# Merged transposes and V loads, a two-pass value product, and a re-ranked instruction order in a thresholded attention and mixer kernel

## The chip, the cores and the metric

The kernel runs on one core of one Trainium2 chip. The metric is the device time of that core in microseconds (us); the time of a kernel is the median of its runs. A profile of one execution, taken by the hardware profiler, goes with it. Its span is a little different from the time of an unprofiled run.

Engines are named as in the profile: PE is TensorE's matmul part and PEld its weight loads, DVE is VectorE, ACT is ScalarE, POOL is GpSimd, SP is the synchronisation engine, which here only issues transfers.

## The reference

There are two parts. The first is attention with a threshold, for 8 batches of 8 heads, 576 rows and 64 columns a head, in fp32:

```python
scores = scale * np.matmul(q, k.transpose(0, 1, 3, 2))
thresh = np.max(scores, axis=-1, keepdims=True) - tau
scores = np.where(scores >= thresh, scores, -1e9)
attn = np.exp(scores - np.max(scores, axis=-1, keepdims=True))
attn = attn / (np.sum(attn, axis=-1, keepdims=True) + 1e-09)
x = np.matmul(attn, v)          # heads side by side: 576 x 512 a batch
```

The second is a mixer on each batch's `x`: a low-rank map over the 576 rows, `u = x + (U V)^T x` (rank 32), and a two-layer perceptron over the 512 columns, `out = u + relu(u W1) W2` with 2048 hidden columns.

## The kernel before, in words

**Tiling.** Two heads make a pair (64 + 64 columns fill the 128 partitions), 4 pairs a batch, 32 pairs in all. Rows come in tiles of 128; 576 = 4 x 128 + 64, so the last 64 rows of two neighbouring pairs share a fifth tile. This gives 9 score steps for two pairs and 144 in all (18 a batch).

**A score step** (`score_tasks`) computes the fp32 scores of one tile for two heads (L423, into two double PSUM banks). VectorE moves them out with the scale and their extreme (L439), ScalarE makes the threshold (L452) and the exponential (L460), VectorE selects and sums (L468) into one of 8 `w_ring` buffers. The weights must then be turned round for the value product. Most are turned by a transfer that SP issues (`turn`, L479); for the fifth tile it issues two, one for the 64 rows of each pair (L482), into columns 512 to 576 of each pair's `wT_ring` buffer. A few tiles are turned by PE with a copy by ScalarE (L487, L496).

**The value product** (`value_tasks`, L551) multiplies the turned weights with V, which is kept as two bf16 halves side by side, high and low (`vh`, L385 and L388). One matmul of 128 columns thus gives 64 columns of the high product and 64 of the low. ScalarE copies the low part out (L574), VectorE adds the high part (L578), GpSimd multiplies by the inverse of the sums (L585). Then come the low-rank map (L602, L617, L624) and the turning of `u` for the perceptron (L632, L641, L649).

**The perceptron** (`mixer_tasks`) of a batch is 16 up-products of 4 matmuls (L716) with a relu (L706), and for each row tile 4 groups of 4 down-products (L749), a sum (L758) and two stores (L771, L772). The fifth tiles of two batches are done together (L732, L775).

**Loads** (`load_tasks`). Q, K and V of a pair come as separate transfers per head and per half of the partitions, so V takes four (L322, L323; all are issued at L305). SP issues V's for the first batch, GpSimd afterwards. GpSimd also issues the weights W1 and W2 in 8 pieces each (L805, L808), cast to bf16 on the way, and all stores.

**The order.** No instruction is scheduled by hand. The class `Order` builds a static order for each engine: every piece of work is a `Task` with an engine, a cost, dependencies, an offset `off`, and for mixer work a due time `when`, counted in score steps. `run` walks a model of the engines and of two transfer queues and, at each point, takes among the tasks that could start within `PATIENCE` of the earliest the one with the smallest rank:

```python
def rank(c):
    s, t = c
    if t.when is not None:
        due = t.when <= steps + (1.0 if t.kind == kind else 0.0)
        return (t.when - 1000.0 if due else t.when + 1000000.0, s)
    return (t.ready + t.off, s)
```

So mixer work comes first once it is due and last before. Where the model sees PE idle for over 0.45 us it puts in matmuls on a tile of zeros (`fill`, L255). A weight piece can't be issued before the first score output of its own step, which `gate` names: W1 at steps 6, 8, ... 20 and W2 at 22, 24, ... 36 (L821, L823). The engines carry out the resulting lists strictly in order: a wait of one instruction holds all behind it on its engine.

Of the kernel before, what the change touches and what calls it, by code (L numbers as in the profile page):

```python
# [8 lines left out]
P = 128  # L9
# [11 lines left out]
HB = 64  # L21
NT = 5
NPAIR = H // 2
NP = B * NPAIR
EARLY = 8

# [15 lines left out]
class Task:  # L42
    __slots__ = ("engine", "cost", "fn", "deps", "off", "banks", "frees", "lag", "kind", "when", "dma",
                 "ndma", "steps",                  "left", "after", "ready", "at", "end", "got")

    def __init__(self, engine, cost, fn, deps=(), off=0.0, banks=0, frees=(), lag=0.0, kind=None,
                 when=None, dma=0.0, ndma=1, steps=0):
        self.engine, self.cost, self.fn = engine, cost, fn
        self.deps = [d for d in deps if d is not None]
        self.off, self.banks, self.frees, self.lag, self.kind = off, banks, frees, lag, kind  # L50
        self.steps = steps
        self.dma = dma
        self.ndma = ndma
        self.when = when
        self.after, self.ready, self.end, self.got = [], 0.0, None, []


class Order:
# [3 lines left out]
    PATIENCE = (0.15, 0.45, 0.15, 0.15, 0.15)  # L62
# [3 lines left out]
    LANDING = (3.0, 1.4)  # L66
    SWITCH = {"quadrants": 0.145, None: 0.095}
    PARTS = {"S": "quadrants"}

    def __init__(self, nbanks, filler):  # L70
        self.tasks, self.nbanks, self.filler = [], nbanks, filler

    def add(self, *args, **kw):
        t = Task(*args, **kw)
        self.tasks.append(t)
        return t

    def run(self):
# [11 lines left out]

# [13 lines left out]
        while left:  # L104
# [37 lines left out]
            at[e] = s + t.cost  # L142
            t.at, t.end = s, at[e] + t.lag
            if t.dma:
                q = e != POOL
                begin = max(moved[q], at[e] + 0.6)
                shared = min(t.dma, max(0.0, moved[1 - q] - begin))
                moved[q] = begin + t.dma + shared
                moved[1 - q] += shared
                t.end = moved[q] + self.LANDING[q]  # L150
                if not q:
                    lanes += [t.end] * t.ndma
# [14 lines left out]
def kernel(  # L167
# [50 lines left out]
    wT_ring = [wpool.tile([P, NT, 2, 640], BF16, name=f"wT_ring{n}") for n in range(2)]  # L218
    for t_ in wT_ring:
        nc.gpsimd.memset(t_[:, :, :, S:640], 0.0)  # L220
    vraw_ring = [wpool.tile([P, NT, 2, D], FP32, name=f"vraw_ring{n}") for n in range(2)]
    for t_ in vraw_ring:
        nc.gpsimd.memset(t_[HB:P, 4, :, :], 0.0)
# [41 lines left out]
    def head_rows(src, b, hp):  # L265
        return src[b, 2 * hp:2 * hp + 2].rearrange("j (p t) d -> p t j d", p=HB)
# [21 lines left out]
    def load_tasks(p, pr):  # L288
# [5 lines left out]
        def one(kind, e, part, to, of, j, deps):  # L294
            queue = {SP: nc.sync, SCA: nc.scalar, POOL: nc.gpsimd}[e]

            def fn(_):
                if kind == "v":
                    raw = pr.vraw
                else:  # L300
                    if pr.qkraw is None:
                        pr.qkraw = rawpool.tile([P, 9, 2, D], FP32, name="qkraw", tag="qkraw")
                    raw = pr.qkraw
                src = {"q": qv, "k": kv, "v": vv}[kind]
                queue.dma_start(raw[part, to, j, :], src[:, of, j, :])  # L305

            return add(e, 0.7, fn, deps, dma=0.2 if e == POOL else 0.35, off=20.0 if p else -9.0)
# [11 lines left out]
        for j in range(2):  # L319
            freed = [got("vlo", p - 2)]  # L320
            ev = SP if p < NPAIR else POOL
            loads["v"].append(one("v", ev, lo, slice(0, 5), slice(0, 5), j, freed))  # L322
            loads["v"].append(one("v", ev, hi, slice(0, 4), slice(5, 9), j, freed))  # L323
# [21 lines left out]
    def prepare_tasks(p):  # L345
# [3 lines left out]
        for x, (name, t0) in enumerate((("q", 0), ("k", 5))):  # L349
# [5 lines left out]
            task = add(PE, 0.44, turn_main, loads[name] + before, off=-2.0, banks=1, kind="qk")  # L355

            def copy(_, x=x, task=task):
# [5 lines left out]
            done[name + "T", p] = add(SCA, 0.55, copy, [task, got(name + "T", p - 1)], off=-1.0,  # L363
# [5 lines left out]
        task = add(PE, 0.11, turn_rest, loads["q"] + loads["k"] + before, off=-2.0, banks=1,  # L369
# [9 lines left out]
        done["qk4T", p] = add(SCA, 0.22, copy_rest, [task, got("qk4T", p - 1)], off=-1.0,  # L379
# [3 lines left out]
        def high(_):  # L383
            pr.vh = vpool.tile([P, NT, 2, 2, D], BF16, name="vh", tag="vh")
            nc.scalar.copy(out=pr.vh[:, :, :, 0, :], in_=pr.vraw)  # L385

        def low(_):
            nc.gpsimd.tensor_tensor(out=pr.vh[:, :, :, 1, :], in0=pr.vraw,  # L388
# [3 lines left out]
                                 loads["v"] + [got("AV", p - 2, g) for g in range(3)] + [got("vhi", p - 1)],  # L392
                                 off=3.0)
# [7 lines left out]
    def score_tasks(p, i):  # L401
# [8 lines left out]
        now = -20.0 if p < NPAIR else 0.0  # L410
# [20 lines left out]
        S_ = done["S", p, i] = add(PE, 0.97, scores, deps, off=now - 6.0, kind="S", steps=1)  # L431
# [4 lines left out]
        for x in range(2):  # L436
            def weigh(_, x=x):
# [6 lines left out]
            t = add(VEC, 0.69, weigh, [S_, got("w", tiles[0] + x - NS)],  # L444
                    off=now - 3.0 + 0.01 * x)
            done["P1", n, x] = t
            if x == 0 and n in gate:
                gate[n].deps.append(t)
# [6 lines left out]
        thr = add(SCA, 0.2, threshold, mins, off=now - 7.0)  # L455

        for x in range(2):
# [5 lines left out]
            ex = add(SCA, 0.73, exponential, [mins[x], got("w", tiles[0] - NS)], off=now - 4.0)  # L463

            def select(_, x=x, w_sb=w_ring[tiles[0] % NW]):
# [8 lines left out]
                VEC, 0.77, select, [ex, thr, got("wT", tiles[0] - NW), got("rec", p - 4)],  # L474
                off=now - 1.0)

            def turn(_, x=x, w_sb=w_ring[tiles[0] % NW]):
                if i < 4:
                    nc.sync.dma_start_transpose(pr.wT[:, :, x, i * P:(i + 1) * P], w_sb[:, :])  # L479
                else:  # L480
                    for a in two:
                        nc.sync.dma_start_transpose(a.wT[:, :, x, 512:S], w_sb[a.part4, :])  # L482
# [7 lines left out]
            free = [got("AV", a, c) for a in (p - 2, p - 1)[:2 if i == 4 else 1] for c in range(3)]  # L490
            if i < 4 and (x == 1 and p < EARLY and i >= 2 or p == NPAIR - 1 and i == 3):
                t = done["wT", tiles[0]] = add(PE, 0.28, turn_pe, [sel] + free, off=now - 1.0, banks=1,
# [8 lines left out]
                t = add(SCA, 0.68, copy_w, [t], off=now - 1.0, frees=[t])  # L501
            else:
                t = done["wT", tiles[0]] = add(SP, 1.2 if i < 4 else 2.4, turn, [sel] + free,
                                               off=now, dma=1.0)
# [5 lines left out]
        if i == 4:  # L510
# [5 lines left out]
            done["den4", p + 1] = add(SP, 0.6, sums, [sel, got("rec", p - 3)], dma=0.1)  # L516


    def value_tasks(p):
        pr = pairs[p]  # L520

        now = -20.0 if p < NPAIR else 0.0
        bt = pr.batch
# [7 lines left out]
        rec = done["rec", p] = add(VEC, 0.37, inverse, [done["den", p], got("den4", p)], off=now + 1.0)  # L531
# [8 lines left out]
        for g, tiles_ in enumerate(((0, 1), (2, 3), (4,))):  # L540
            n = len(tiles_)

            def product(t, tiles_=tiles_):

                av = bank[t.got[0]].rearrange("p (a m) -> p a m", m=P)
                for a, i in enumerate(tiles_):

                    lo = i * P if i < 4 else S - P if bt.odd else 512
                    for j in range(2):
                        for kt in range(NT):  # L550
                            nc.tensor.matmul(av[:, 2 * a + j, :], pr.wT[:, kt, j, lo:lo + P],  # L551
                                             pr.vh[:, kt, j, :, :], start=(kt == 0),
                                             stop=(kt == NT - 1))

            av = done["AV", p, g] = add(
                PE, 0.56 * n, product,
                done["wTs", p, g] + [done["vlo", p], got("AV", p - 1, g)],
                off=now - 1.0, banks=1, kind="AV")

            def rows(g=g):  # L560
# [3 lines left out]
                return bt.h4, bt.x4[bt.h4, pr.cols].rearrange("p (t j d) -> p t j d", t=1, j=2)  # L564

# [14 lines left out]
            t = add(SCA, 0.36 if n == 2 else 0.28, low_part, [av] + opens, off=now - 2.0)  # L580
            t = add(VEC, 0.35 if n == 2 else 0.22, join, [t], off=now - 2.0, frees=[av])

            def norm(_, g=g, n=n, rows=rows):
                part, x = rows()
                nc.gpsimd.tensor_tensor(  # L585
                    out=x, in0=x, in1=pr.rec[part, 2 * g:2 * g + n, :].unsqueeze(3).to_broadcast(
                        [part.stop - part.start, n, 2, D]), op=ALU.mult)

            xs.append(add(POOL, 0.7 if n == 2 else 0.4, norm, [t, rec], off=now - 4.0))

        def narrow(_):
# [4 lines left out]
        xb = done["xb", p] = add(SCA, 0.8, narrow, xs + [got("tt_", p - 2), got("xb", p - 1)],  # L596
                                 off=now - 1.0)
# [7 lines left out]
        tt_ = done["tt_", p] = add(PE, 0.3, low_rank, [xb, weights0[0]], off=now - 3.0, banks=1, kind="lr")  # L605
# [4 lines left out]
        tt = done["tt", p] = add(SCA, 0.2, copy_tt, [tt_], off=now - 3.0, frees=[tt_])  # L610
# [9 lines left out]
        h = done["h", p] = add(PE, 0.23, spread, [tt, weights0[1]], off=now - 3.0, banks=1, kind="h")  # L620
# [7 lines left out]
        u = add(VEC, 0.62, sum_u, [h], off=now - 1.5, frees=[h])  # L628

        def narrow_u(_):  # L630
# [3 lines left out]
        ub = done["ub", p] = add(SCA, 0.57, narrow_u, [u, got("uT_", p - 2), got("ub", p - 1)],  # L634
                                 off=now - 1.0)

        def turn(t):
# [6 lines left out]
        uT_ = done["uT_", p] = add(PE, 0.23, turn, deps, off=now - 3.0, banks=1, kind="uT")  # L644
# [231 lines left out]
```

## Time and profile before

| | |
|---|---|
| time, median of 3 runs | 649.67 us (647.91 to 653.22) |
| span of the profiled execution | 653.6 us |
| PE matmul busy | 612.9 us, 94%, 6074 records |
| PE weight load busy | 358.0 us, 55% |
| DVE busy | 532.4 us, 81% |
| ACT busy | 471.2 us, 72% |
| POOL busy | 411.4 us, 63% |
| transfers | 87.61 MB, mean 134 GB/s |
| chain that ended last | PE 71%, DMA 10%, DVE 7%, ACT 4%, issue 4%, POOL 3% |
| costliest: exponential (L460), select (L468), score output (L439) | 220.7, 245.0, 206.1 us |
| scores (L423), up (L716), down (L749), value product (L551) | 183.7, 117.1, 127.4, 105.6 us |
| POOL issues of Q, K and V (L305) | 82.3, 81.9 and 73.6 us, about 0.66 us each |

The chain is followed back from the last instruction: at each step to what released it or to the instruction before it on its engine. "DMA" in it is time between the issue of a transfer and its landing. The page's slices divide the span into 40 equal parts; a digit is the busy share in tenths. PE and DVE are both near full over much of the span, so what matters is which of the two sets the pace in which stretch. Fillers (L255) count as busy PE though they compute nothing.

### The profile page before, as it was taken

What the parts mean: (1) busy time and instruction counts of PE and PEld (TensorE: products, weight loads), DVE (VectorE), ACT (ScalarE), POOL (GpSimd) and SP (SyncE); (2) the same over time, 40 slices, a digit from 0 to 9 for tenths busy, and PEclk for the clock granted to TensorE, in tenths of its full rate; (3) what the DMA queues carried; (4) which work ended last, traced back from release to release, by engine and by line L of the source; (5) the groups of instructions that cost most, each with busy time, mean ns of one, the idle gap of its engine ahead of it and who ended that gap; (6) DMA issues with size and microseconds to landing.
All of it is one profiled execution on the core that took longest, in us unless ns stands there. A gap on an engine that the chain in (4) does not pass through costs nothing.

```text
span 653.6 us, 16904 instructions
## 1 busy us (share of the span) xinstructions
PE 612.9 (94%) x6074; PEld 358.0 (55%) x6153; DVE 532.4 (81%) x1399; ACT 471.2 (72%) x987; POOL 411.4 (63%) x604
## 2 busy tenths in 40 slices
PE   8898899894999999999999999999999999999996
PEld 3455555452565566556655566556555566655452
DVE  4999898893999989988999989988999989984101
ACT  5587788793777886878678876878678877766330
POOL 9875995680768487856768496856767593412111
PEclk9999999896999999999999999999999999999998
DMA  6999999998699999988999889969897878653202
GB/s 143 157 159 163 145 171 132 160 150 97 123 153 158 124 158 162 146 127 143 154 153 169 133 140 163 157 128 140 152 158 153 137 143 125 114 97 49 48 19 62
DMA packets 213171, 87.61 MB, mean 134 GB/s; under 512 B 199008, under 2 KB 203952, under 8 KB 213088
## 3 DMA queue, kind: packets, MB, share of 16 engines
q1 hardware_dynamic: 190224, 45.86, 53.0%
q0 software_dynamic: 21984, 40.46, 31.7%
q8 instruction: 48, 0.79, 0.5%
q14 instruction: 35, 0.29, 0.2%
q10 hardware_dynamic: 880, 0.21, 0.1%
HBM read 36.86 MB, written 9.44 MB: 71 GB/s over the span
## 4 chain that ended last, share of the span: by engine, by line
PE 71%; DMA 10%; DVE 7%; ACT 4%; issue 4%; POOL 3%; POOLq 0%; DVEq 0%; ACTq 0%
PE scores L423 19%; PE bank L749 17%; PE bank L716 15%; PE bank L551 10%; DMA wT_ring<-w_ring 9%; DVE w_ring L468 3%; PE bank L352 3%; PE bank L732 2%; DVE s_sb L439 2%; ACT e_sb L460 2%; POOL qkraw L305 1%; PE bank L602 1%; PE bank L641 1%; PE bank L617 1%; DVE rec L527 1%
## 5 line engine op out<-in xcount | busy, mean ns | idle before, releaser
L460 ACT ACTIVATE e_sb<-s_sb,m 128x576 bf16<-128x576 f32 x288 | 220.7, 768 | 70.4 <-DVE s_sb L439 69.4
L468 DVE SCALAR_TENSOR_TENSOR w_ring<-s_sb,thr,e_sb 128x576 bf16<-128x576 f32 x288 | 245.0, 875 | 10.9 <-ACT thr L452 6.5
L439 DVE TENSOR_SCALAR_CACHE_REDUCE s_sb<-scores 128x576 f32<-128x576 f32 x288 | 206.1, 752 | 52.7 <-PE scores L423 50.4
L423 PE MATMUL scores<-qkT 64*64 64x288 f32 x2304 | 183.7, 417 | 2.5 <-DVE s_sb L439 2.4
L585 POOL TENSOR_TENSOR x<-x,rec 64x128 f32<-64x128 f32 (+1 forms) x96 | 75.0, 784 | 141.8 <-DVE x L578 93.8
L749 PE MATMUL bank<-W2b,R 128*128 128x512 bf16 x540 | 127.4, 379 | 3.5 <-issue 2.4
L551 PE MATMUL bank<-vh,wT_ring 128*128 128x128 bf16 x1600 | 105.6, 220 | 18.0 <-DMA wT_ring<-w_ring 16.3
L716 PE MATMUL bank<-uT,W1b 128*128 128x512 bf16 x478 | 117.1, 383 | 3.0 <-issue 1.2
L423 PEld LDWEIGHTS scores<-qkT 64*64 64x64 f32 x2304 | 80.0, 132 | 64.1 <-DVE s_sb L439 13.6
L551 PEld LDWEIGHTS <-wT_ring 128*128 128x128 bf16 x1600 | 93.6, 98 | 36.3 <-DMA wT_ring<-w_ring 18.0
L305 POOL DMA_DIRECT2D qkraw<-in_q_dram x125 | 82.3, 664 | 30.2 <-PE bank L367 17.8
L706 ACT ACTIVATE R<-bank 128x512 bf16<-128x512 f32 x144 | 80.4, 589 | 23.1 <-PE bank L716 12.2
L749 PEld LDWEIGHTS <-R 128*128 128x128 bf16 x576 | 53.6, 98 | 68.9 <-issue 11.0
L305 POOL DMA_DIRECT2D qkraw<-in_k_dram x125 | 81.9, 661 | 3.1 <-DMA vraw_ring<-in_v_dram 1.1
L716 PEld LDWEIGHTS <-W1b 128*128 128x128 bf16 x512 | 47.7, 99 | 64.5 <-issue 15.3
L305 POOL DMA_DIRECT2D vraw_ring<-in_v_dram x112 | 73.6, 662 | 4.3 <-POOL vh L388 2.4
L758 DVE TENSOR_TENSOR o<-bank,x 128x512 f32<-128x512 f32 x36 | 24.7, 686 | 42.3 <-PE bank L749 42.1
L360 ACT COPY qkT<-bank 128x512 f32<-128x512 f32 x64 | 35.4, 581 | 21.0 <-PE bank L352 20.5
L388 POOL TENSOR_TENSOR vh<-vraw_ring,vh 128x640 bf16<-128x640 f32 x32 | 45.0, 1406 | 6.7 <-ACT vh L385 4.1
L574 ACT COPY x<-bank 128x256 f32<-128x256 f32 (+1 forms) x96 | 31.4, 328 | 21.3 <-PE bank L551 20.7
L771 POOL DMA_DIRECT2D out_dram<-o x32 | 18.3, 573 | 43.4 <-DVE o L758 43.4
L452 ACT ACTIVATE thr<-m,tau_t 128x2 f32<-128x2 f32 x144 | 40.5, 281 | 5.5 <-DVE s_sb L439 5.5
(67 smaller groups left out, 523.4 us busy)
## 6 DMA issues: line engine op xcount, KB each, us to landing
out_dram<-o POOLq DMA_DIRECT2D x72, 128.0 KB, 3.1
qkraw<-in_k_dram POOLq DMA_DIRECT2D x63, 80.0 KB, 4.5
qkraw<-in_q_dram POOLq DMA_DIRECT2D x62, 80.0 KB, 4.6
wT_ring<-w_ring SPq DMA_TRANSPOSE x303, 4.2
vraw_ring<-in_v_dram POOLq DMA_DIRECT2D x56, 80.0 KB, 3.4
qkraw<-in_q_dram POOLq DMA_DIRECT2D x63, 64.0 KB, 4.2
qkraw<-in_k_dram POOLq DMA_DIRECT2D x62, 64.0 KB, 4.4
vraw_ring<-in_v_dram POOLq DMA_DIRECT2D x56, 64.0 KB, 3.3
```

Source lines behind the costliest of these rows:

```text
L305: queue.dma_start(raw[part, to, j, :], src[:, of, j, :])
L388: nc.gpsimd.tensor_tensor(out=pr.vh[:, :, :, 1, :], in0=pr.vraw, in1=pr.vh[:, :, :, 0, :], op=ALU.subtract)
L423: nc.tensor.matmul(pair_bank[j][part, c, 0:HC], a.tT[hs, 0, rows], a.tT[hs, 1, cs], start=True, stop=True)
L439: nc.vector.tensor_scalar(out=s_sb.rearrange("p (a c) -> p a c", a=2), in0=pair_bank[x][:, :, 0:HC], scalar1=-scale, scalar2=None, op0=ALU ...
L452: nc.scalar.activation(out=st["thr"], in_=st["m"], func=ACT.Identity, bias=tau_t[:, 0:1], scale=1.0)
L460: nc.scalar.activation(out=st["e", x], in_=st["s", x], func=ACT.Exp, bias=st["m"][:, x:x + 1], scale=-1.0)
L468: nc.vector.scalar_tensor_tensor(out=w_sb[:, 0:S], in0=st["s", x], scalar=st["thr"][:, x:x + 1], in1=st["e", x], op0=ALU.is_le, op1=ALU.mu ...
L551: nc.tensor.matmul(av[:, 2 * a + j, :], pr.wT[:, kt, j, lo:lo + P], pr.vh[:, kt, j, :, :], start=(kt == 0), stop=(kt == NT - 1))
L585: nc.gpsimd.tensor_tensor(out=x, in0=x, in1=pr.rec[part, 2 * g:2 * g + n, :].unsqueeze(3).to_broadcast([part.stop - part.start, n, 2, D]), ...
L706: nc.scalar.activation(out=R2[:, fts, lo:hi], in_=bank[t.got[0]].rearrange("p (f c) -> p f c", c=hi - lo), func=ACT.Relu)
L716: nc.tensor.matmul(bank[t.got[0]], W1b[:, dt, ft * P:(ft + 1) * P], bt.uT[:, dt, :], start=(dt == 0), stop=(dt == 3))
L749: nc.tensor.matmul(ch, R2[:, ft, lo:lo + P], W2b[:, ft, :], start=(ft == 0), stop=(ft == 15))
```

## The change

It has four parts.

1. The fifth tile's weights are turned by one transfer for both pairs, into a buffer of their own, `wT4` (256 columns, of which the transfer fills 64 to 192; the rest stays zero). The value product reads a window of 128 columns of it that puts the wanted pair's rows into the right half. Transposes of whole tiles now wait for two of the three value products of the pair two before, and the fifth tile's only for the third of both pairs before.
2. V of a pair is loaded by two transfers in place of four, each with both heads; `vraw_ring` has the head ahead of the row tile for that, and the reads of it are rearranged.
3. For the 4 pairs of the first batch (`SOFT = 4`) the high and low products are added in PSUM: two matmuls of 64 columns in place of one of 128. ScalarE's copy and GpSimd's product fall away, and VectorE multiplies by the inverse as it reads PSUM.
4. The order. The model's figures for transfers are changed (costs of loads, landing times, how two queues share), `PATIENCE` is zero but on DVE and POOL (indices 1 and 3), the offsets come from a table by kind of task and phase (first batch, middle, last batch), found by a search offline, and the weight pieces' steps and the mixers' due times are lists. PE's list as built holds 66 fillers, before 92; POOL's holds 522 rows, before 600, and SP's 300, before 340.

The core of the diff:

```diff
+SOFT = 4
+W1_AT = (11, 12, 12, 13, 13, 14, 14, 15)
+W2_AT = (19, 20, 21, 22, 23, 24, 25, 26)
+DUE = (30, 48, 66, 104, 129, 161, 178, 201)
...
-    PATIENCE = (0.15, 0.45, 0.15, 0.15, 0.15)
+    PATIENCE = (0, 0.3, 0, 0.2, 0)
...
-    LANDING = (3.0, 1.4)
+    SHARE = (0.5, 0.5)
+    LANDING = (1.8, 0.9)
...
+    OFF = {
+        "copy_main": (-1, -4, -1), "copy_rest": (-1, -1, 19), "copy_tt": (-23, -14, -3),
...
+        t.off = self.OFF[t.fn.__name__][self.phase]
...
-            at[e] = s + t.cost
+            at[e] = s + t.cost * (1.0, 1.02, 1.02, 1.05, 1.0)[e]
...
-                shared = min(t.dma, max(0.0, moved[1 - q] - begin))
-                moved[q] = begin + t.dma + shared
-                moved[1 - q] += shared
+                other = max(0.0, moved[1 - q] - begin)
+                share = self.SHARE[q]
+                moved[q] = begin + min(t.dma / share, t.dma + other)
+                moved[1 - q] += min(t.dma, other * share / (1 - share))
...
-    wT_ring = [wpool.tile([P, NT, 2, 640], BF16, name=f"wT_ring{n}") for n in range(2)]
-    vraw_ring = [wpool.tile([P, NT, 2, D], FP32, name=f"vraw_ring{n}") for n in range(2)]
+    wT_ring = [wpool.tile([P, NT, 2, 512], BF16, name=f"wT_ring{n}") for n in range(2)]
+    wT4 = wpool.tile([P, NT, 2, 256], BF16, name="wT4")
+    vraw_ring = [wpool.tile([P, 2, NT, D], FP32, name=f"vraw_ring{n}") for n in range(2)]
...
-                if i < 4:
-                    nc.sync.dma_start_transpose(pr.wT[:, :, x, i * P:(i + 1) * P], w_sb[:, :])
-                else:
-                    for a in two:
-                        nc.sync.dma_start_transpose(a.wT[:, :, x, 512:S], w_sb[a.part4, :])
+                to = pr.wT[:, :, x, i * P:(i + 1) * P] if i < 4 else wT4[:, :, x, HB:HB + P]
+                nc.sync.dma_start_transpose(to, w_sb[:, :])
...
-            free = [got("AV", a, c) for a in (p - 2, p - 1)[:2 if i == 4 else 1] for c in range(3)]
+            free = [got("AV", p - 2, c) for c in range(2)] if i < 4 else \
+                [got("AV", a, 2) for a in (p - 2, p - 1)]
...
+                            for h in range(2):
+                                nc.tensor.matmul(av[:, 2 * a + j, :], w, pr.vh[:, kt, j, h, :],
+                                                 start=first and h == 0, stop=last_ and h == 1)
...
+                    nc.vector.tensor_tensor(out=x, in0=made, in1=over_sum(part), op=ALU.mult)
...
-        due = 18 * (b + 1) + 12
+        due = DUE[b]
...
-                    when=due + 9 * ft / 16)
+                    when=due + 6.75 * ft / 16)
...
-                        kind="p1", when=due + 9 + 2 * g)
+                        kind="p1", when=due + -94.25 + 5.25 * g)
...
-                when = due + 22 if i == 4 and b < B - 1 else due + 9 + 9 * (i + g / 4) / 4
+                when = due + 113 if i == 4 and b < B - 1 else due + 16.75 + 6.25 * (i + g / 4) / 4
```

Due times above 144 never come within the 144 score steps: such mixer work is taken only where nothing else on PE can start.

## The prediction

> **What bounds the kernel now.** I read the page first, then a table by stage (one stage a row: busy time of the five engines, clock, DMA share, GB/s), then the waits, then the chain of waits in order of time. In the page's slices TensorE is full from about 180 us on and patchy before:
>
> ```profile
> PE   8898899894999999999999999999999999999996
> DVE  4999898893999989988999989988999989984101
> POOL 9875995680768487856768496856767593412111
> PEclk9999999896999999999999999999999999999998
> ```
>
> The cuts of the table are 9 us (first score step), 97 (step 24 of 144), 141 (step 36), 179 (step 42) and 588 (the last one is done). Those times are starts in the score matmul's group: 9.2, 96.8, 141.3, 178.6; its last record is at 587.1.
>
> ```profile
> 9.00:97.00 88.00, 77.58 (x840) 45.48 (x852) 81.48 (x210) 66.17 (x140) 72.55 (x108) 1.00 1.07 158
> 97.00:141.00 44.00, 38.73 (x415) 22.37 (x413) 39.14 (x109) 36.19 (x76) 29.53 (x41) 0.96 1.06 139
> 141.00:179.00 38.00, 28.16 (x270) 16.58 (x278) 26.58 (x72) 22.70 (x49) 18.16 (x27) 0.87 0.84 125
> 179.00:588.00 409.00, 403.32 (x4162) 239.57 (x4208) 369.95 (x973) 319.05 (x677) 270.65 (x381) 1.00 0.89 143
> 588.00:654.00 66.00, 58.38 (x380) 31.10 (x384) 13.53 (x28) 24.35 (x46) 12.12 (x23) 0.97 0.23 45
> ```
>
> Three regimes. Up to 141 us VectorE is busy 120.6 of 132 us (91.4%): it sets the pace, 3.7 us a step, while TensorE fills gaps with idle matmuls (L255, 23.3 us, nearly all before 100 us). From 141 to 179 everything stops once. From 179 us TensorE is busy 403 of 409 us and sets the pace; after 588 us it works off the last mixer almost alone. The stop is one wait:
>
> ```profile
> PE bank L551 <- DMA wT_ring<-w_ring: 16.3, 8, 9.4
> DVE s_sb L439 <- PE scores L423: 50.4, 60, 10.7
> ```
>
> The value matmul waits once for 9.4 us for transposed weights; scores stand behind it in TensorE's order, so VectorE then waits 10.7 us. The timeline shows the cost of the matmuls after it, 2.20 us for a score step that takes 1.13 us elsewhere:
>
> ```profile
> 157.80 1.25 PE L551 MATMUL bank<-vh,wT_ring 128*128 128x128 bf16 x10 [9.42 <-DMA wT_ring<-w_ring]
> 158.84 0.74 PE L487 MATMUL bank<-identb,w_ring 128*128 128x128 bf16 x5
> 159.51 2.20 PE L423 MATMUL scores<-qkT 64*64 64x288 f32 x16
> ```
>
> **What the Trainium skill says.** (1) "TensorE: Matmul & The Clock Gate", Part 1, says an idle window of about 3.4 us halves TensorE's clock. The trace agrees: granted clock 0.87 in the stage with the stop, and the doubled score step above. (2) The same page, Back-to-back issue gap, has a stream of weight-load and matmul pairs at about 81 ns each for 128 columns, and says matmuls of 1 to 64 columns do not scale down below their issue floor. The trace differs on the first: 20 value matmuls in 1.22 us, 61 ns. No run here shows 64 columns. (3) "DMA: Bandwidth & Descriptors", Queues, rings and completion order, says each DMA engine takes turns between queues that have work. So weight, q/k/v and transpose transfers share the engines; the trace's DMA share above 1.0 up to 141 us agrees that they compete there.
>
> **The change, part by part.**
>
> *Value products of the first batch (4 pairs).* 200 matmuls of 128 columns become 400 of 64, each with its own weight load. If a short one costs half of 61 ns the edit adds nothing, if all of it, 200 x 61 ns = 12.2 us. I take 12.2: the weight load is as long as before. It lies in the stage where VectorE sets the pace, and beside it 26 fewer idle matmuls are issued (92 to 66 in the built order, 26 x 0.22 = 5.7 us), so it costs the end nothing. Gone are 12 ScalarE copies (L574, 328 ns, 3.9 us) and 12 GpSimd products (L585, 784 ns, 9.4 us); VectorE's 12 sums become 12 products of like size: zero.
>
> *Last rows' transposes.* 64 half transposes (1204 ns of SP time each) become 32 whole ones. At the whole form's 1220 ns SP saves 38 us in all; at worst a whole one takes two halves and it saves nothing. The bytes are the same, so DMA time is not saved. SP is in order: at 132 us the trace shows four halves (5.08 us) and the row sums' transfer (1.98 us) in front of nine whole ones, and the transfer TensorE then waited for was issued at 146.19 and landed 11.56 us later. Two fewer issues are 2.5 us less queue. The buffer wT4 is single: its transposes wait for the third value product of both pairs before. The old ones waited for those products too, so no new wait.
>
> *V loads.* 112 GpSimd issues at 662 ns become 56, saving 56 x 0.66 = 37 us of GpSimd if a double one costs the same, nothing if twice. GpSimd is 72.55 of 88 us busy in the first stage and on the chain there from 65.8 to 82.8 us, behind q/k loads. There it helps; after 179 us it is hidden by TensorE. I give it and the SP saving together 4 us before step 36, bounded by 0 and the 11.4 us that VectorE is idle there.
>
> *Order and weight loads.* I counted the matmuls before each score step in the built orders and priced them from the chain: score step 1.13 us, 512-column matmul 0.216 (16 of L749 in 3.45), 128-column bf16 0.061, fp32 transpose 0.109. Before: 110.9 us of work precede step 42, 575.6 in all. After: 131.7 and 587.8. So more is done while VectorE sets the pace, and 456.1 us are left at step 42 in place of 464.7. Before, from 178.6 us to TensorE's last record at 647.2, 464.7 us of work took 468.6 us, a factor 1.008. After: 456.1 x 1.008 = 459.8, 8.8 us less. From there VectorE has to keep up with the same steps in less time: it was at 370/409 = 90%. For steps in which it is the later of the two I add 3 us, bounds 0 and 9.
>
> The W1 and W2 pieces, 16 of 256 KB landed, are now gated to steps 11 to 26 instead of 6 to 36. W1 pieces landed in 5.3 us, W2 in 6.5 (medians). The burst ends before the first up-products, and the 9.4 us stop came under a W2 piece issued at 144.87. I take it that 10 of the 14.5 us that this stage is over a normal six steps (37.3 against 22.8) go, bounds 0 and 14.5: the transfers still queue somewhere.
>
> **Sum.** -10 (stop) -4 (early pace) -8.8 (work moved forward) +3 (VectorE pressure) = -20 us on 649.67, which gives 630 us. Cheapest ends: stop and pace together can't bring step 42 below VectorE's floor (156 us, rival B), -22.6 -8.8 +0 = -31, 618 us. Dearest without a new stop: 0 0 -8.8 +9 = 0, 650 us.
>
> **The rivals.**
> *A, the stop moves with the weights:* 16 pieces in half the steps with the DMA share already at 1.07 delay transposes around 50 to 100 us as W2 did at 146. The stop stays and only the moved work and a few us of pace show: -8.8 +3 +3, about 647 us. For it: the DMA share. Against it: the weights are done before 105 us, when TensorE has no mixer work and its gaps cost little.
> *B, the early stage was held by GpSimd and the queue more than I allow:* step 42 comes at VectorE's floor, 9 us plus the 147.2 us that it was busy, at 156 us: -22.6 -8.8 = 618 us. For it: GpSimd on the chain at 66 to 83 us. Against: VectorE never ran above 93% of a stage.
> *C, slower:* the burst gives two stops of 14.5 us in addition to the old one's share, and the narrower margin costs 9: +29 -8.8 +9 -10, about 669 us. For it: the in-order engines pass one late transfer on to all. Against: 12 us of slack from fewer idle matmuls and 46 us of GpSimd time.
>
> **How the numbers follow.** Forecast 0.62, A 0.18, B 0.10, C 0.10. The time is the forecast's, 630 us. The range takes the bounds, 618 to 650: it holds the forecast, B and most of A and leaves out C. Faster by over 1% means below 643 us: the forecast, B and a little of A, 0.76; within 1%: most of A, 0.14; slower: C, 0.10.
>
> **What would show it.** Step 42 should start near 164 us (178.6 before), with no wait of TensorE on a transpose over 4 us and no clock under 0.95 between 140 and 180 us. TensorE should stay over 98% busy from there to the end, the last record some 60 to 65 us after the last score step. Value matmuls of 64 columns should stand at about 60 ns each in the chain. V issues should stay under 0.8 us each, whole last-row transposes at 1.2 us of SP. I am wrong if a wait on transposes appears between 50 and 110 us, if VectorE stays at 91% with step 42 beyond 175 us, or if TensorE falls below 97% after it.

## The result, and the profile after

The changed kernel takes 641.42 us (640.70 to 643.21), the kernel before 650.0 us beside it. The ratio is 0.9868, with a 95% interval of 0.9821 to 0.9914: 8.6 us or 1.3% faster. The forecast was 20 us, so the direction was right and the size was more than twice too large. Times here and below are medians of all executions, while ratios leave out executions over 1.5% longer than the same kernel's fastest, so the two can differ where the times are spread.

The page's slices of the changed kernel show the place. TensorE is full from the eighth slice on (112 us), but there is a new hole in the fifth (64 to 80 us), where the granted clock falls too (its digit is 6):

```profile
PE   7998488999999999999999999999999999999995
DVE  2999497989988899999998999999989899993101
POOL 9865254447878677757746576767576633322102
PEclk7999699999999999999999999999999999999999
```

The table by stage of the changed kernel (columns as before: busy time of TensorE, its weight loads, VectorE, ScalarE and GpSimd, then clock, DMA share and GB/s). The cuts are its first score step, steps 24, 36 and 42, and the last score step:

```profile
13.00:105.00 92.00, 77.32 (x1029) 46.56 (x1025) 77.97 (x211) 62.56 (x126) 53.77 (x77) 0.93 0.98 145
105.00:155.00 50.00, 47.87 (x483) 26.66 (x486) 42.53 (x118) 41.17 (x84) 22.53 (x32) 0.97 0.81 125
155.00:182.00 27.00, 26.99 (x328) 17.93 (x324) 26.23 (x65) 22.81 (x48) 20.82 (x31) 1.00 0.82 147
182.00:571.00 389.00, 387.98 (x4074) 225.56 (x4070) 360.40 (x964) 317.15 (x668) 247.47 (x342) 1.00 0.96 149
571.00:641.00 70.00, 63.83 (x413) 33.10 (x413) 16.36 (x34) 25.42 (x48) 13.66 (x26) 0.99 0.28 58
```

Set against the first table, the difference of the two profiled spans (653.6 and 641.4 us, -12.2) splits into two parts that I had not expected to have these signs:

| | before | after | difference | forecast |
|---|---|---|---|---|
| first score step starts | 9.2 us | 12.8 us | +3.6 | 0 |
| step 18 | 72.1 | 82.0 | +9.9 | |
| step 42 | 178.6 | 181.7 | +3.1 | -14.6 |
| step 42 to TensorE's last record | 468.6 | 453.1 | -15.5 | -5.8 |
| from there to the end | 6.4 | 6.6 | +0.2 | 0 |

The old stop (148 to 158 us) is gone: TensorE is busy for 26.99 of the 27 us before step 42. But step 42 comes no sooner, because step 18 is already 10 us late. The new stop is again a wait for transposed weights. These are the longest waits of TensorE and of VectorE between 51 and 82 us (who waited <- for whom: us in total, times, longest):

```profile
PE bank L584 <- DMA wT_ring<-w_ring: 8.5, 2, 7.1
DVE x L607 <- PE bank L584: 7.9, 1, 7.9
DVE s_sb L466 <- PE scores L450: 1.0, 1, 1.0
```

At the old stop VectorE waited for the scores behind the value product (10.7 us). Here it waits for the value product itself: in the first batch it now reads that product directly (part 3 of the change), and this read stands before the next scores in its order.

TensorE's timeline there reads just as the old stop did, with the slow score step behind it:

```profile
68.45 0.76 PE L584 MATMUL bank<-vh,wT_ring 128*128 128x64 bf16 x20 [1.39 <-DMA wT_ring<-w_ring]
76.35 1.25 PE L584 MATMUL bank<-vh,wT_ring 128*128 128x64 bf16 x20 [7.14 <-DMA wT_ring<-w_ring]
77.53 2.20 PE L450 MATMUL scores<-qkT 64*64 64x288 f32 x16
```

In the chain of waits the transfer that ended this has 17.84 us from issue to landing. GpSimd's and SP's timelines show what stood beside it: from 54.9 to 66.2 us GpSimd issued seven of the eight W1 pieces, with two loads of V and two of Q among them, and one SP issue took 5.24 us instead of 1.2:

```profile
54.89 1.11 POOL L846 DMA_DIRECT2D W1b<-in_moe_w_ch_dram  x2
57.19 1.17 POOL L846 DMA_DIRECT2D W1b<-in_moe_w_ch_dram  x2
61.43 0.56 POOL L846 DMA_DIRECT2D W1b<-in_moe_w_ch_dram  x1 [0.47 <-DMA W1b<-in_moe_w_ch_dram]
```

```profile
63.39 1.21 SPq L505 DMA_TRANSPOSE wT<-w_ring  x1
64.69 2.69 SPq L537 DMA_DIRECT2D d_ring<-d_ring  x1
67.47 5.24 SPq L505 DMA_TRANSPOSE wT<-w_ring  x1
```

The transfer queues between 60 and 70 us (packets, MB, share of the 16 transfer engines' time) show who got the engines: the queue that GpSimd feeds 94%, the queue with the transposes 18%.

```profile
q0 software_dynamic: 753, 1.50, 94.2%
q1 hardware_dynamic: 944, 0.23, 18.1%
```

My theory after this result: the weight burst stops the early stage, and the rest of the change gains about what was forecast. Rivals: the two-pass product, SP's queue, or the new order as such.

### The profile page after: what moved, and what is told of

Read it like the earlier page. It is cut to its first block, busy times and chain, and to the rows that moved or that the text cites. A ratio compares the mean times of both kernels' runs of the same rounds, so it can differ in the third digit from the quotient of the medians.

```text
span 641.4 us, 17146 instructions
## 1 busy us (share of the span) xinstructions
PE 612.5 (96%) x6327; PEld 353.7 (55%) x6327; DVE 526.8 (82%) x1399; ACT 472.6 (74%) x975; POOL 370.4 (58%) x535
## 4 chain that ended last, share of the span: by engine, by line
PE 83%; DMA 8%; DVE 5%; issue 2%; ACT 1%; POOL 1%; POOLq 0%; DVEq 0%; ACTq 0%
PE scores L450 22%; PE bank L790 20%; PE bank L757 16%; PE bank L580 12%; DMA wT_ring<-w_ring 7%; PE bank L379 4%; DVE w_ring L495 3%; PE bank L773 2%; DVE s_sb L466 2%; PE bank L646 1%; PE bank L661 1%; PE bank L394 1%; PE bank L684 1%; DMA qkraw<-in_k_dram 1%; PE bank L283 1%
## 5 line engine op out<-in xcount | busy, mean ns | idle before, releaser
L495 DVE SCALAR_TENSOR_TENSOR w_ring<-s_sb,thr,e_sb 128x576 bf16<-128x576 f32 x288 | 241.3, 861 | 5.2 <-ACT thr L479 2.8
L790 PE MATMUL bank<-W2b,R 128*128 128x512 bf16 x576 | 137.9, 379 | 0.0
L632 POOL TENSOR_TENSOR x<-x,rec 128x256 f32<-128x256 f32 (+1 forms) x84 | 68.9, 823 | 105.3 <-DVE x L625 53.4
L757 PE MATMUL bank<-uT,W1b 128*128 128x512 bf16 x512 | 124.6, 381 | 0.0
L747 ACT ACTIVATE R<-bank 128x512 bf16<-128x512 f32 x144 | 83.2, 592 | 23.3 <-PE bank L757 16.9
L416 POOL TENSOR_TENSOR vh<-vraw_ring,vh 128x640 bf16<-128x640 f32 x32 | 48.2, 1506 | 54.9 <-ACT vh L412 54.5
L580 PE MATMUL bank<-vh,wT_ring 128*128 128x128 bf16 x1120 | 72.5, 219 | 3.1 <-DMA wT_ring<-w_ring 3.1
L580 PEld LDWEIGHTS <-wT_ring 128*128 128x128 bf16 x1120 | 64.9, 98 | 17.7 <-issue 10.1
L479 ACT ACTIVATE thr<-m,tau_t 128x2 f32<-128x2 f32 x144 | 41.7, 290 | 8.1 <-DVE s_sb L466 7.5
L379 PE MATMUL bank<-ident,qkraw 128*128 128x128 f32 x256 | 36.1, 279 | 3.2 <-DMA vraw_ring<-in_v_dram 2.8
L347 POOL DMA_DIRECT2D vraw_ring<-in_v_dram x56 | 34.5, 621 | 4.0 <-POOL vh L416 2.7
```

What stands on the lines that cost most here:

```text
L379: nc.tensor.transpose(bank[t.got[0]][:, i * P:(i + 1) * P], pr.qkraw[:, t0 + i, :, :], ident)
L495: nc.vector.scalar_tensor_tensor(out=w_sb[:, 0:S], in0=st["s", x], scalar=st["thr"][:, x:x + 1], in1=st["e", x], op0=ALU.is_le, op1=ALU.mu ...
L580: nc.tensor.matmul(av[:, 2 * a + j, :], w, pr.vh[:, kt, j, :, :], start=first, stop=last_)
L632: nc.gpsimd.tensor_tensor(out=x, in0=x, in1=over_sum(part), op=ALU.mult)
L747: nc.scalar.activation(out=R2[:, fts, lo:hi], in_=bank[t.got[0]].rearrange("p (f c) -> p f c", c=hi - lo), func=ACT.Relu)
L757: nc.tensor.matmul(bank[t.got[0]], W1b[:, dt, ft * P:(ft + 1) * P], bt.uT[:, dt, :], start=(dt == 0), stop=(dt == 3))
```

## The experiments

Each was timed beside the kernel before, which took 649.2 to 650.2 us. "Same order" means that the order of the instructions on each engine is that of the kernel it starts from. "Order built anew" means that the planner, given the edited tasks, made another one.

**The weights cut to an eighth, same order.** W1's pieces load 128 of 1024 columns, and in a second kernel W2's 64 of 512 too. The rest is zero.

```diff
-            cs = slice(h * (F // 2), (h + 1) * (F // 2))
+            cs = slice(h * (F // 2), h * (F // 2) + F // 16)
...
+    nc.vector.memset(W1b, 0.0)
```

> The changed kernel, same order on every engine, but each of the 8 W1 pieces loads only 128 of its 1024 columns (the rest of W1 is a zero fill by VectorE at the start), so part of the weights is left out. Theory 1 (the burst of W1 transfers at steps 11 to 15 starves the transposes): TensorE's waits on transposes between 51 and 82 us fall from 8.5 us to under 2, step 18 starts near 72 us (82.0 in the changed kernel), and the time falls from 641.4 to about 632 us. Theory 2 (the stop comes from SP's in-order queue, from the two-pass value product or from the order itself): the stop stays at 7 us or more and the time within 3 us of 641.

> As the one with W1 cut to an eighth, and W2's pieces cut to 64 of 512 columns too (zero filled), order unchanged. Theory 1: the second wait, 8.6 us for a transpose at 101 us, shrinks as well, steps 12 to 36 run at VectorE's pace, step 42 starts near 165 us (181.7 in the changed kernel) and the time is about 626 to 630 us. Theory 2: both waits stay, 638 us or more.

Measured: 630.42 us (ratio 0.9665, 0.961 to 0.9719) and 630.73 us (0.9671, 0.9617 to 0.9725). In the profile with W1 cut (an execution of 636.6 us), TensorE has no wait on a transpose between 51 and 82 us. Step 18 starts at 71.5 us and step 42 at 172.8. The queues between 60 and 70 us have changed places:

```profile
q1 hardware_dynamic: 2771, 0.66, 51.7%
q0 software_dynamic: 704, 0.61, 33.3%
```

Theory 1 holds for W1: without most of its bytes the time is 11 us shorter. W2's burst costs nothing further here. The 8.6 us at 101 us in the second forecast is the flight of a transfer in the chain; TensorE waited only 2.1 us for it.

**The weights spread, order built anew.**

```diff
-W1_AT = (11, 12, 12, 13, 13, 14, 14, 15)
-W2_AT = (19, 20, 21, 22, 23, 24, 25, 26)
+W1_AT = (6, 8, 10, 12, 14, 16, 18, 20)
+W2_AT = (22, 23, 24, 25, 26, 27, 28, 29)
```

> The changed kernel with W1 pieces at steps 6, 8, ... 20 as before the change and W2 at 22 to 29; the order is built anew from that. Theory 1: no TensorE wait on a transpose above 4 us between 50 and 85 us, time 632 to 637 us. Theory 2: the time stays at 641 us within 3, since weights are not what stops it. A third way: the stop moves to W2 at 100 to 150 us, as in the kernel before, and the time stays at 641.

Measured: 642.08 us (0.9866, 0.9797 to 0.9935), the number of Theory 2 but not its reason. In the profile, of an execution of 648.5 us, step 42 does come at 171.6 us, 10 us sooner, but from there TensorE needs 468.5 us, not 453.1. The planner reacts to the moved pieces with another order on every engine, and the offsets were searched for with the old steps. What spreading gains, the new order seems to lose, so the two are separated below.

**One pass in the first batch again, order built anew** (`SOFT = 0`).

> The changed kernel with the one-pass value product in the first batch as before the change (SOFT = 0), order built anew. If the two-pass product costs the end nothing, as predicted: 641 us within 3. If it is part of the stop, because VectorE now waits for TensorE directly in the product by the inverse (7.9 us at 69.7 us): 633 to 637 us. If it is what gained in the early stage (less ScalarE and GpSimd work): 645 us or more.

Measured: 653.89 us (1.0054, 1.0033 to 1.0075), slower than both kernels. TensorE waits 12.0 us for transposes between 51 and 85 us (8.5 in the changed kernel), and needs 465.1 us after step 42. As in the run before, the built order changed too (122 fillers, not 66), so this does not price the two-pass product by itself. It suggests that the offsets fit one set of tasks.

**The second pass left out, same order.** The low half of V is left out of the first batch's product.

```diff
-                            for h in range(2):
-                                nc.tensor.matmul(av[:, 2 * a + j, :], w, pr.vh[:, kt, j, h, :],
-                                                 start=first and h == 0, stop=last_ and h == 1)
+                            nc.tensor.matmul(av[:, 2 * a + j, :], w, pr.vh[:, kt, j, 0, :],
+                                             start=first, stop=last_)
```

> The changed kernel, same order on every engine, but the first batch's value product leaves its second pass (the low half of V) out: 200 matmuls of 64 columns fewer. If the second pass is hidden in the early stage, as predicted: 641 us within 2. If it lies on the path: up to 12 us less, 629 to 635 us.

Measured: 643.77 us (0.993, 0.9906 to 0.9953), no gain. The second pass is hidden, in a kernel that still has the new stop (a wait of 7.7 us ending at 75 us).

**V in four transfers again, same order** (each issue made two).

> The changed kernel, same order on every engine, with V loaded by four transfers a pair again (one a head), two issues where one was. Theory of the prediction (37 us of GpSimd time, hidden by TensorE after 180 us, worth at most a few us before): 641 to 644 us. Rival (GpSimd held the early stage): 648 us or more. Each issue about 0.66 us, so GpSimd's issues of V about 74 us in all (34.5 in the changed kernel).

Measured: 643.75 us (0.9928, 0.9903 to 0.9954). That is 2.3 us more than the changed kernel, and the two intervals overlap: at most a small gain, as forecast.

**The fifth tile's transposes in halves again, same order.**

```diff
+                for c in (0, HB):
+                    nc.sync.dma_start_transpose(wT4[:, :, x, HB + c:P + c], w_sb[c:c + HB, :])
```

> The changed kernel, same order on every engine, with each fifth-tile transpose issued as two of 64 rows into the two halves of wT4 (64 issues again in place of 32). Theory of the prediction (SP's queue gives only a small part of 4 us early, nothing later): 641 to 645 us. Rival (SP's in-order queue is what the transposes stand in, so 38 us of SP time matter): 648 us or more, with longer waits of TensorE on transposes. Other rival (it costs nothing, since the bytes are the same): 641 us within 1.

Measured: 657.8 us (1.0113, 1.0047 to 1.0179), 16 us slower than the changed kernel and slower than the kernel before. I had allowed 4 us for this part together with another. The profile is of an execution of 664.4 us (the other three took 651.9 to 661.0), so it shows where time can go and not how much in the median. After step 42, where the changed kernel's TensorE waits 1.0 us for transposes, this execution waits 11.4 us (columns as above):

```profile
PE bank L583 <- DMA wT<-w_ring: 5.9, 3, 4.1
PE bank L583 <- DMA wT_ring<-w_ring: 5.5, 8, 1.4
```

**The merge alone, same order as the kernel before.** This is the kernel before with one transpose for both pairs into `wT4` and nothing else.

> The kernel before the change, same order and planner costs, with the fifth tile's weights turned by one transfer into wT4 (part 1 of the change alone). If the merge is worth what splitting it again cost in the changed kernel (16 us): 634 to 640 us. If it matters only where the order leaves TensorE no slack: 646 to 650 us. By the prediction's 4 us for SP and GpSimd together: 646 to 650 us.

Measured: 640.93 us (0.9869, 0.9849 to 0.9889). One part of four gives what all four give together. TensorE's wait of 9.4 us is gone, step 42 comes at 163.7 us (178.6), and the stage that held the stop now reads, for the kernel with the merge:

```profile
141.00:179.00 38.00, 37.10 (x389) 22.82 (x396) 36.43 (x96) 31.07 (x67) 23.93 (x36) 1.00 0.97 156
```

TensorE is busy for 37.10 us of 38, where in the kernel before it is for 28.16. Steps 36 to 42 take 26.5 us in place of 37.3. From step 42 on it needs 468.5 us, as before. The merge also takes the fifth tile out of `wT_ring`; the run with halves kept `wT4`, so splitting costs without that too.

**Parts 1 to 3 with the old offsets, due times and weight steps, order built anew.**

> The kernel before the change with parts 1 to 3 (merged transposes, merged V loads, two-pass value product in the first batch) and its own offsets, due times and weight steps. If the parts bring the gain and the new order little: 638 to 643 us. If the order brings it: 646 to 650 us. If the parts without the weight burst avoid the stop at 58 us and keep the gain: 632 to 637 us.

Measured: 644.41 us (0.9921, 0.9898 to 0.9943), 3.5 us more than with the merge alone. With the old offsets the merged V loads and the two passes together do not gain, but the order on every engine is another one, so this does not price them. The first score step starts at 11.7 us here, against 9.0 with the merge alone.

**The old kernel with W2 cut to an eighth, same order.**

> The kernel before the change, same order, with each W2 piece loading only 64 of its 512 columns (the rest zero filled by VectorE at the start; part of the weights is left out). Theory 1 (its stop at 146 us is a transpose starved by a weight piece): TensorE's 9.4 us wait is under 3 us, step 42 starts near 167 us (178.6 before), and the time is 637 to 641 us. Theory 2 (the backlog in SP's queue and the q/k loads make it): the wait stays over 6 us and the time at 647 us or more.

Measured: 645.23 us (0.9942, 0.9928 to 0.9957), between the two theories. The wait shrinks from 9.4 to 3.6 us and step 42 comes at 169.6 us. The old stop thus had two conditions, the weight pieces and the split transposes. Taking either away shortens it; only the merge ends it. The old kernel with its weights moved earlier and nothing else was not run.

**The weights spread in the same order.** The planner keeps the changed kernel's plan; only the place of the 16 issues in GpSimd's list is other. A second kernel also fills only the two zero strips of `wT4`.

```diff
+ISSUE = dict(enumerate((6, 8, 10, 12, 14, 16, 18, 20, 22, 23, 24, 25, 26, 27, 28, 29)))
...
+            while later and (e == POOL and t.dma and later[0][0] <= steps or later[0][1] <= steps):
+                later.pop(0)[2](None)
```

```diff
-    nc.gpsimd.memset(wT4, 0.0)
+    for c in (0, P + HB):
+        nc.gpsimd.memset(wT4[:, :, :, c:c + HB], 0.0)
```

> The changed kernel with the same order on every engine, but the 16 weight issues put elsewhere in GpSimd's list: W1 at steps 6, 8, ... 20, W2 at 22 to 29. The run that spread the weights and built the order anew reached step 42 at 171.6 us (181.7 in the changed kernel) but lost it later (468.5 us from there, 453.1 in the changed kernel). Theory 1 (burst at the start, order later): step 42 near 172 us, 453 to 456 us from there, time 631 to 635 us. Rival (the stop only moves): 641 us within 3.

> The same with only the two zero strips of wT4 filled by GpSimd at the start, not all of it (2.2 us becomes about 1.3). The first scores start at 10 to 11 us in place of 12.8. If VectorE sets the early pace from its first work on: 1 to 2 us less than the run without it. If the late start is made up by step 12, as in the changed kernel: no difference.

> The changed kernel, same order, with only the two zero strips of wT4 filled at the start. If the late first score (12.8 us in place of 9.2) is part of what was missed: 638 to 640 us. If it is made up by step 12: 641 us within 1. If the strips made the difference between the two spread runs: 635 us or less.

> The changed kernel in the same order with the weight issues spread (W1 at steps 6 to 20, W2 at 22 to 29) and the strips of wT4 alone filled, again. If the gain is the spread: 631 to 635 us. If the first result was chance, like the unspread run at 639.7 us: 637 to 641 us.

Measured:

| | time | ratio to before | step 42 | from there |
|---|---|---|---|---|
| changed kernel | 641.42 | 0.9868 (0.9821 to 0.9914) | 181.7 | 453.1 |
| strips | 638.31 | 0.9807 (0.9767 to 0.9846) | 177.8 | 453.3 |
| spread | 639.70 | 0.9767 (0.9705 to 0.9829) | 180.5 | 453.0 |
| spread and strips | 631.39 | 0.9705 (0.9672 to 0.9739) | 169.2 | 453.1 |
| the same again | 633.84 | 0.9752 (0.9712 to 0.9792) | 170.8 | 454.6 |

Spread and strips together beat both kernels, and the late stage is untouched by either. The spread alone is not settled. Its four times lie between 631 and 646 us, its ratio rests on two of them (631 and 638), and its profile is of one that took 642 us, with 26 us for steps 6 to 12 (20 in the changed kernel).

The strips alone are not settled either. Their time is 3.1 us below that of the changed kernel, but the two intervals overlap. The timelines at the start, first of the changed kernel and then of the one with strips, show that the short fill lets GpSimd issue its first load 1.0 us sooner:

```profile
1.91 2.22 POOL L248 MEMSET wT<- 128x2560 bf16 x1
2.06 2.16 DVE L219 CAST identb<-ident 128x128 bf16<-128x128 f32 x1
4.49 0.77 POOL L329 DMA_DIRECT2D qkraw<-in_q_dram  x1
```

```profile
1.91 1.20 POOL L249 MEMSET wT<- 128x640 bf16 x2
2.06 1.13 DVE L219 CAST identb<-ident 128x128 bf16<-128x128 f32 x1
3.46 0.77 POOL L330 DMA_DIRECT2D qkraw<-in_q_dram  x1
```

The first scores start at 10.8 us in place of 12.8. But step 18 comes at 81.4 us, against 82.0: most of the head start is used up at the stop. And the kernel with W1 cut takes 630.42 us with the full fill. So no run shows that the full fill costs time at the end.

The stage table of the kernel with spread and strips, up to step 24 and from step 42 to its last score step (169 to 559 us):

```profile
11.00:95.00 84.00, 74.50 (x1018) 45.90 (x1025) 77.80 (x210) 62.50 (x125) 53.54 (x76) 1.00 1.04 156
...
169.00:559.00 390.00, 385.68 (x4028) 225.93 (x4087) 361.40 (x964) 318.18 (x671) 247.76 (x343) 1.00 0.98 149
```

VectorE is busy for 93% of the first stage (85% in the changed kernel), and the clock granted there is 1.00 (0.93). In the profile of the second run it is 0.86 between 50 and 75 us, so some of the stop may remain.

**The burst on top of the merge, old offsets, order built anew.**

> The kernel before with the merged transposes alone (640.9 us, no stop, step 42 at 163.7 us), and the weight pieces gated as in the change: W1 at steps 11 to 15, W2 at 19 to 26; offsets and due times as before the change. If the burst starves the transposes in any order: TensorE waits 5 us or more on a transpose between 50 and 110 us, step 42 later than 170 us, time 647 to 653 us. If it does so only in the new order: 639 to 643 us.

> A second profile of the merged transposes with the weight burst in the old order, whose times were spread from 641 to 654 us and whose first profile (span 644.5 us) shows no wait on a transpose over 2 us. If the burst stops some executions and not others: in a profile of 648 us or more, TensorE waits 5 us or more on a transpose between 50 and 110 us; in one under 645 us it does not.

Measured: the 20 times lie between 640.65 and 654.47 us (median 650.72), so most are longer than without the burst (640.47 to 641.79). Both profiles fell among short executions (spans 644.5 and 641.6 us). In them the eight W1 pieces are issued from 50.5 to 66.4 and from 48.6 to 64.5 us, almost as in the changed kernel (49.2 to 65.7), and yet no wait on a transpose between 50 and 110 us is over 2.0 us. So the burst alone does not make the stop in every order or execution; what the changed kernel's order adds to it is open. Nor does a profile show what makes the long executions long. The order differs from the one with the merge alone, and in both profiles TensorE needs 472.5 us after step 42, 4 us more, with no weights left to load.

**What the merge relieves, same order.** Behind each merged transpose come two small transfers (SP's time without bytes), or one transpose of 16 rows (the number of transposes without most of the bytes).

```diff
+                    for c in range(2):
+                        t_ = spare[(2 * x + c) % 4]
+                        nc.sync.dma_start(t_[0:HB, :], t_[HB:P, :])
```

```diff
+                    nc.sync.dma_start_transpose(spare[x][:, :, :], w_sb[0:16, :])
```

> The kernel before with the merged transposes alone, and behind each of the 32 merged ones two spare transfers of 0.5 KB on SP's queue, so that SP's time is given back (two issues of 0.5 to 1 us for the half transpose of 1.2 us) but hardly any bytes. If SP's queue is what the merge relieves: the stop comes back, step 42 after 172 us, time 646 to 651 us. If it is the transfers' own work: 640 to 643 us.

> The kernel before with the merged transposes alone, and behind each merged one a further transpose of 16 rows into a spare tile: 64 transposes on the fifth tiles again, with an eighth more bytes there in place of none. If a transpose has a price of its own, whatever its rows: the stop comes back, step 42 after 172 us, time 646 to 652 us. If only its bytes and SP's time count: 642 to 644 us, as with the spare transfers.

Measured: 643.16 us (0.9898, 0.9866 to 0.993) and 640.39 us (0.9872, 0.9827 to 0.9917). The small transfers gave 38.9 us of SP's time back, of the 51 us that the merge saves (404.6 us of SP's issue time for transposes before, 353.7 with the merge), and the time is 2.2 us longer, which the intervals do not tell from nothing. The further transposes gave even more of it back (41.7 us) and cost nothing. So neither SP's time nor the number of transposes is the main part of the 8.7 us.

What remains is how a half moves, and that is open. In the kernel before, a half lands 3.5 us after its issue (median), and with the merge a whole one 4.3 us: a half takes far more than half the time. In the changed kernel with halves it even takes 4.3 us, where a whole one takes 4.2. No run shows that this is the cause.

## Why the prediction was right or wrong

**"-10 (stop)": right in size, mostly wrong in cause, and then given back.** This is the failed step. Steps 36 to 42 took 37.3 us and now take 27.0, so the 10 us came. But the prediction credited them to the weights coming earlier. The merge gives them alone, with the weights where they were (26.5 us); fewer bytes of W2, without the merge, give about half (32.0). The weights coming earlier did harm: in the changed kernel's order the W1 burst made a stop of its own, and cutting W1 to an eighth saves 11 us. Step 42 therefore gained nothing (181.7 us against 178.6).

Rival A said this, down to the range of 50 to 100 us, and the prediction had named a wait on transposes there as a sign of being wrong. It was given 0.18 because TensorE "has no mixer work and its gaps cost little" there. TensorE's gap did not matter for TensorE, but VectorE, which sets the pace there, stood too: its product by the inverse waits on that TensorE work directly (7.9 us). I had followed the wait on to VectorE for the old stop and not for the new place.

**"-4 early pace": wrong.** Even with spread and strips, steps 0 to 36 take 130.8 and 132.3 us (two profiles), against 132.1 before, and they start 2.2 us later (11.4 and 9.2 us). The late start had been put at nothing; with the full fill of `wT4` it is 3.6 us. And the reason was wrong in kind: SP's share was priced by issues saved (2.5 us of queue). The merge is worth 8.7 us with the old order and splitting it again costs 16 us in the new one, but giving most of SP's time back costs 2.2 us in one run and nothing in the other.

**"-8.8 (work moved forward) +3 (VectorE pressure)": right in kind, too small.** From step 42 to TensorE's last record the change is -15.5 us. 12.0 us of it are moved work, by the prediction's own prices of matmuls. I had counted 8.6 by a slip: I took the work up to the end of the 42nd score step and the time from its successor's start. Counted at the start of step 42, 460.0 us of work were left before and 448.0 after. The other 3.5 us are idle or slow time that is gone. TensorE is busy for 387.98 of 389 us (99.7%; 98.6% before), so the feared pressure of VectorE did not come, though VectorE is at 360/389 = 93%.

**"The edit costs the end nothing" (two passes): right.** It is 643.8 us without the second pass. My 12.2 us for TensorE's part was at the wrong end of its bounds. In the chain 20 matmuls of 64 columns with their weight loads take 0.61 us, 30 ns each, where 128 columns take 61. Two short ones cost what one long one did. The Trainium skill, "TensorE: Matmul & The Clock Gate", Back-to-back issue gap, on which I leaned for the high end, puts the issue floor of 1 to 64 columns near 25 ns. The trace's 30 ns is near that figure and far from the 61 ns that I read into it. In rival C, the 12 us of slack from fewer idle matmuls are not in my own count either, which gives 5.7.

**"V loads, hidden by TensorE": right.** Splitting them again costs 2.3 us, which the intervals do not tell from nothing. An issue of twice the size takes 621 ns, against 662 before.

**The sum.** With the burst spread and the strips alone filled, the same order takes 631 to 634 us, near the 630 forecast. So the W1 burst covers up about half of what this order can give; whether the zero fill has a part in it is open. That the sum then meets the forecast is partly luck: step 42 comes at 169 to 171 us, where 164 was forecast, and the stage after it is 8 to 10 us shorter than forecast.

## What to carry to other kernels

When an edit moves transfers, ask at the new place the question that explained the old stop: which in-order engine waits for the transfers beside them, and who stands behind it. An engine's own slack does not make its wait cheap. And when a planner orders the work, test an edit inside a kept order first; in two orders built anew the time after step 42 was 12 and 15 us longer here, far from the edit, which hid what the edit did.

## What was not expected of the hardware

- Between 60 and 70 us of the changed kernel the GpSimd-fed queue with the weight pieces had 94% of the transfer engines' time and the transposes 18%. A transpose issued just before then took 17.8 us to land, where the median is 4.2. SP's issue of one stretched from 1.2 to 5.24 us.
- VectorE's cast of 128x128, which starts 0.15 us after a GpSimd fill, took 2.16 us beside the fill of 2560 elements (2.22 us). Beside two fills of 640 (0.6 to 0.7 us each) it took 0.56 us in the kernel before and 1.13 in the changed kernel with strips. It ended each time within 0.1 us of the end of a fill.
- 32 further transposes of 16 rows, 41.7 us of SP's issue time, cost no time, while splitting 32 whole ones in halves cost 16 us.
